# A mixed attention and feed-forward kernel on one core: half of the feed-forward weight loads move to GpSimd's queue

## The chip, the core and the metric

The kernel runs on one core of a Trainium2 chip. Its engines are TensorE (PE, with weight loads shown apart as PEld), VectorE (DVE), ScalarE (ACT), GpSimd (POOL) and SyncE (SP). SP, ACT and POOL can each issue DMAs; all DMAs run on the core's 16 DMA engines. The metric is the device time of one execution in microseconds (us). Times in the profile are counted from the start of the profiled span.

## What is computed

One input x of 2048 rows by 640 columns (bf16) goes through two branches, which a gate mixes per row.

```python
g = _sigmoid((x * gate_w).sum(-1, keepdims=True))
a = _A_ref(x, A_wqkv, A_w_phi, A_wo)      # linear attention, 32 heads of 20
b = (_gelu(x @ w_gate) * (x @ w_up)) @ w_down      # 640 -> 1728 -> 640
return g * a + (1 - g) * b
```

In the attention branch q, k and v come from `x @ wqkv`. q and k go through a 20 by 20 matrix per head (`w_phi`) and then through two softmaxes, of the result and of its negative, so that each head has 40 features. The sums over the rows of features times v, and of the features alone, give numerator and denominator of each row's output, which `wo` maps back to 640 columns.

## The kernel before

**Tiling.** Rows are taken in 16 tiles of 128 and in 4 blocks of 512. The 1728 columns of the feed-forward branch are 13 chunks of 128 and a tail of 64, whose gate and up halves share one tile `wt`. `chunk(b, c)` makes five matmuls of 512 columns with `wg` and five with `wu` (L647), applies GELU on ScalarE (L661) and multiplies on VectorE (L663) into `hT`. `down_tile` (L935, L944) adds the products with `w_down` and those of the attention with `wo` for one tile of rows.

**Startup.** `startup` (L446) loads everything. The first 512 rows of x come as rows (`xtok`) and are transposed on TensorE (`tile`, L559) and copied out by ACT or DVE (L593, L595); the other three blocks of x (`x_t`), and the columns of wqkv that belong to k and q (`w_t`, giving `WkT` and `WT`, six transposes each), come through DMA transposes on SP (L454). `spin` (L550) issues products of zeros on TensorE whose result nobody reads: 18 before the first x tile, five before the first weights. Chunks 0 and 1 of block 0 are made in two halves of 256 rows, because x arrives in parts; chunks 2 to 4 follow with 512 columns.

**The fold.** `w_phi` is folded into the weights of k and q. `masks` (L606) builds, on GpSimd, the block-diagonal matrices `BD` of six groups of six heads from `w6` (the loaded `w_phi`) and the mask `BM`. `fold_m` (L621) multiplies `WkT` (or `WT`) by `BD`: a first half needs groups 0 to 2, a second groups 3 to 5. The results go to `wK` (`wQ`), and `half` (L687) then makes k, v and q of one tile of rows in two halves of 320 columns. `wV` is loaded as it is, with the gate vector as a 641st column; `grow` is the gate vector as five rows, transposed at L573.

**Order.** The kernel does not stand in the order in which it is written. Each step is recorded by `_Prog.op` with an engine, an estimated duration, a priority and what it reads and writes; `schedule` then lays out a queue for each engine from these estimates, and `emit` writes the instructions with semaphore waits. Reads and writes in SBUF are compared in cells of 32 bytes (`CELL`). `TIMES` holds the priorities of the later stages (written as due times), `HOLD` how long a switch of ScalarE's function table is put off. On each engine the instructions run in the order so found, and a waiting instruction holds all that is queued behind it on that engine.

**DMA queues.** Before the change every load is issued by SP, but for the gate row (ACT) and `w_down` and `wo`, which GpSimd issues once the last transpose of `WT` has landed (`after=(tr,)`). In the wait lists a DMA's semaphore belongs to a lane of its queue; SP has 24 lanes, GpSimd 8.

**SP's order before:** two tiles of x, gate and up columns 0 to 256, two tiles of x, gate and up columns 256 to 640, the larger piece of w_phi, six WkT transposes, the smaller piece of w_phi, wV, gate and up columns 640 to 1152, and then transposes of x, between which the remaining gate, up and tail columns stand.

Of the kernel before, what the change touches and what calls it, by code (L numbers as in the profile page):

```python
# [7 lines left out]
P = 128  # L8
# [24 lines left out]
class _Prog:  # L33
# [70 lines left out]
        return o  # L104


    HOLD = 3.9

    def schedule(self):
        ops = self.ops  # L110
# [160 lines left out]
class _Kernel:  # L271
    S, D, H, F = 2048, 640, 32, 1728
    DH, KD, NT, NB, TB, BT = 20, 5, 16, 4, 4, 512
    NG, HPG = 6, 6
# [14 lines left out]
    def alloc(self):  # L289
        nc = self.nc  # L290
        T = nc.alloc_sbuf_tensor
        D, S, KD = self.D, self.S, self.KD
        self.ident = T("ident", [P, P], BF)
        self.KVM = T("KVM", [P, 6, 21], BF)
        self.KV = T("KV", [P, self.NCH, 63], BF)
        self.gcol = T("gcol", [P, self.NT], F32)
        self.Gr = T("Gr", [P, self.NT], F32)
        self.Gm = T("Gm", [P, self.NT], F32)
        self.xT = T("xT", [P, KD, S], BF)
        self.wo = T("wo", [P, KD, D], BF)  # L300
        self.wg = T("wg", [P, KD, self.FM], BF)
        self.wu = T("wu", [P, KD, self.FM], BF)
        self.wt = T("wt", [P, KD, P], BF)
        self.wd = T("wd", [P, self.NC, D], BF)
        self.hT = T("hT", [P, 2, self.NC, self.BT], BF)
        SW = self.HP * self.DH
        self.Sq = T("Sq", [P, self.NT, SW], BF)
        self.NSK = 4
        self.Sk = T("Sk", [P, self.NSK, SW], BF)
        self.NVA = 6  # L310
        self.vaug = T("vaug", [P, self.NVA, self.HP, self.DH + 1], BF)
        self.NGL = 4
        self.gel = T("gel", [P, self.NGL, self.BT], BF)
        self.NOS = 2
        self.osb = T("osb", [P, self.NOS, D], BF)
        self.NSM = 2
        HB = 2 * self.HP
        self.t1 = T("t1", [P, 2, HB, 10], BF)
        self.t2 = T("t2", [P, 2, HB, 4], BF)
        self.t3 = T("t3", [P, 2, HB, 2], BF)  # L320
        self.m2 = T("m2", [P, self.NSM, 2, HB, 2], BF)
        self.rr = T("rr", [P, self.NSM, 2 * HB], F32)
        self.r2 = T("r2", [P, self.NSM, 2 * HB, 2], BF)
        self.zt = T("zt", [P, 4, 18], F32)
        self.zr = T("zr", [P, 4, 18], F32)

        self.NE = 5
        self.dn = T("dn", [P, self.NE, 2 * self.NCH, 6], F32)
        self.E = T("E", [P, self.NE, 2 * self.NCH, P], BF)
        self.e_slot = {}  # L330
        self.e_of = [None] * self.NE
        self.e_left = {}
        self.e_ring = 0
        self.dn_left = [0] * self.NE

        b0 = nc.lookup_mloc(self.hT).addr + self.NC * self.BT * 2
        W = self.HPG * self.DH
        for name, shape in (("BD", [P, self.NG, W]), ("BM", [P, W]),
                            ("w6", [W, self.NG, self.DH]),
                            ("grow", [KD, P])):  # L340
            setattr(self, name, nc.alloc_sbuf_tensor_at(name, shape, BF, offset=b0))
            b0 += -(-int(np.prod(shape[1:])) * 2 // 64) * 64
        b1 = nc.lookup_mloc(self.Sq).addr
        self.xtok = nc.alloc_sbuf_tensor_at("xtok", [P, self.TB, D], BF, offset=b1)
        self.WkT = nc.alloc_sbuf_tensor_at("WkT", [P, self.NG, D], BF, offset=b1 + self.TB * D * 2)
        self.WT = nc.alloc_sbuf_tensor_at("WT", [P, self.NG, D], BF, offset=b1 + (self.TB + self.NG) * D * 2)
        assert self.TB + 2 * self.NG <= self.NT


        wk = T("wK", [P, KD, D], BF)  # L350
        wv = T("wV", [P, KD, D + 16], BF)
        wq = T("wQ", [P, KD, D], BF)
        self.wP = (wk, wq, wv)
        b2 = nc.lookup_mloc(wk).addr
        kv, end = KD * (2 * D + 16) * 2, KD * (3 * D + 16) * 2

        def inside(name, shape, n, at):
            size = int(np.prod(shape[1:])) * 2
            return [nc.alloc_sbuf_tensor_at(f"{name}{i}", shape, BF, offset=b2 + at + i * size) for i in range(n)]
        pt = self.NCH * P * 2  # L360
        self.phiT = inside("phiT", [P, self.NCH, P], 2, 0)
        self.OT = inside("OT", [P, KD, P], 4, 2 * pt)
        assert 2 * pt + 4 * 1280 <= kv
        self.OT += inside("OTq", [P, KD, P], 2, kv)
        self.phiT += inside("phiTq", [P, self.NCH, P], 1, kv + 2560)
        assert kv + 2560 + pt <= end
        self.O = [T(f"O{i}", [P, D], BF) for i in range(2)]
        self.NO, self.NOT = 2, 6
        self.ps = nc.alloc_psum_tensor("ps", [P, 8 * BANK], F32)
# [24 lines left out]
    def at(self, T, fn, *args):  # L394
# [1 line left out]
        self.todo.append((T, len(self.todo), fn, args))  # L396


    TIMES = dict(wkp=-4.57, dfk=0.51, dfq=0.95, mask=-16.43, fold_k=12.18, t0=33.24, per=21.78, pair=3.13,
                 exp=3.84, ff=14.55, dff=2.71, fold_q=39.04, rest=-4.17, drest=-3.34, q=-38.61, dq=2.39,  # L400
                 qlate=13.99, q0pre=-21.12, q0exp=-8.41, q0post=1.5, at0=31.81, d0=53.28, q1pre=-18.21,
                 q1exp=2.34, q1post=25.29, f2=28.62, df=1.8, at1=10.48, d1=41.89, q2pre=4.15, q2exp=7.74,
                 q2post=13.74, f3=67.06, at2=21.14, d2=90.12, q3pre=-29.71, q3exp=6.32, q3post=17.94, at3=41.36,
                 d3=45.04)

    def plan(self):
        q = self.TIMES
# [38 lines left out]
    def startup(self):  # L446
# [4 lines left out]
        def dma(q, dst, src, prio, nbytes, after=(), transpose=False, dur=0.45):  # L451
            def emit(e):
                if transpose:
                    return e.dma_start_transpose(dst, src)  # L454
                return e.dma_start(dst, src)  # L455
            return pr.op(q, emit, writes=[dst], dur=dur, prio=prio, dma=True, nbytes=nbytes, after=after)
# [19 lines left out]
        pool(lambda e: e.affine_select(bmv, bmv, pattern=[[DH, HPG], [0, DH]], compare_op=ALU.is_ge, fill=0.0,  # L476
                                       base=DH - 1, channel_multiplier=-1), [bm], [bm], 120)

        dma("act", self.grow[:, :], self.gw_d.rearrange("(kt p) -> kt p", p=P), -30.0, 2000)
        for t in range(self.TB):  # L480
            dma("sp", self.xtok[:, t, :], self.x2[t * P:(t + 1) * P, :], -9.0 + t, 163840)
        wg_r = self.wg_d.rearrange("(kt p) n -> p kt n", p=P)
# [1 line left out]
        D2 = 2 * D  # L484
        wr = self.wqkv.rearrange("(kt p) n -> p kt n", p=P)

        def ffn_w(i, a, b):
            n = (b - a) * (1420 if b - a < 512 else 1070)
            dma("sp", self.wg[:, :, a:b], wg_r[:, :, a:b], i, n)
            dma("sp", self.wu[:, :, a:b], wu_r[:, :, a:b], i + 0.01, n)  # L490

        ffn_w(-7.5, 0, 256)
        ffn_w(-4.8, 256, 640)

        wphi = self.wphi.rearrange("h d f -> (h d) f")
        W = HPG * DH
        r = self.rows_g[-1]
        dma("sp", self.w6[:, 0:NG - 1, :], wphi[0:W * (NG - 1), :].rearrange("(g p) f -> p g f", p=W), -4.75, 240000)
        dma("sp", self.w6[0:r, NG - 1, :], wphi[W * (NG - 1):, :], -4.74, 20000)
        wkp = self.TIMES["wkp"]  # L500

        def w_t(dst, col, i):
            for g in range(NG):
                c0 = col + g * HPG * DH
                o = dma("sp", dst[:, g, :], self.wqkv[:, c0:c0 + P], i + 0.001 * g, 400000, transpose=True, dur=1.3)
            return o
        w_t(self.WkT, D, wkp)
        dma("sp", self.wP[2][:, :, 0:D], wr[:, :, D2:3 * D], wkp + 0.009, 657000)
        ffn_w(-4.4, 640, 1152)

        def x_t(b):
            for kt in range(KD):
                dma("sp", self.xT[:, kt, b * 512:(b + 1) * 512], self.x2[b * 512:(b + 1) * 512, kt * P:(kt + 1) * P],
                    -4.3 + 0.1 * b + 0.01 * kt, 380000, transpose=True, dur=1.6)
        x_t(1)
        ffn_w(-4.19, 1152, self.FM)
        dma("sp", self.wt[:, :, 0:64], wg_r[:, :, self.FM:self.F], -4.18, 81920)
        dma("sp", self.wt[:, :, 64:128], wu_r[:, :, self.FM:self.F], -4.17, 81920)
        x_t(2)
        tr = w_t(self.WT, 0, -4.05)  # L520
        x_t(3)
# [32 lines left out]
        def tile(t, prio):  # L554
            bk = self.next_a()

            def tr(e):
# [13 lines left out]
        col = self.wP[2][:, :, D:D + 1].rearrange("p k o -> p (k o)")  # L571
        bg = self.next_a()
        pr.op("pe", lambda e: e.transpose(self.bankb(bg, 8)[:, 0:KD], gr, idk), reads=[gr, idk], writes=[bg], dur=0.1,  # L573
              prio=1.4)
        pr.op("dve", lambda e: e.tensor_copy(col, self.bankb(bg, 8)[:, 0:KD]), reads=[bg], writes=[col], dur=0.1, prio=3.5)
        spin(5, 1.5, (tile(1, 1.0),))
        banks = [(_Bank(True), _Bank(True)) for _ in range(2)]
        for h in range(2):
            if h:
# [18 lines left out]
    def masks(self, p0):  # L598

        W = self.HPG * self.DH  # L600
        bm = self.BM[0:W, :].rearrange("p (j f) -> p j f", f=self.DH)
        for g in range(self.NG):
            dst = self.BD[0:W, g, :].rearrange("p (j f) -> p j f", f=self.DH)
            src = self.w6[:, g, :]
            sb = src.unsqueeze(1).to_broadcast([W, self.HPG, self.DH])
            self.pr.op("pool", lambda e, dst=dst, sb=sb: e.tensor_tensor(dst, sb, bm, ALU.mult),  # L606
                       reads=[src, self.BM[0:W, :]], writes=[dst], dur=0.35, prio=p0)
# [393 lines left out]
```

## Time and profile before

| | |
|---|---|
| median of 3 runs | 293.33 us (291.94 to 294.5) |
| the profiled execution | 294.05 us, of which 291.5 us are the profiled span |
| TensorE busy | 285.8 us, 98% of the span |
| VectorE / ScalarE / GpSimd busy | 210.7 / 160.8 / 11.6 us |
| granted TensorE clock | 1.00 throughout |
| DMA | 24.24 MB in 61739 packets, 52803 of them under 512 bytes |

A page's groups are named by line, engine, operation and tiles; "ps<-xT,wg" is a product of xT and wg written to the accumulator ps. Matmuls are pipelined, so the busy time of a group is not the sum of single durations, and the chain (the work that ended last, followed back) gives the better spacing. For a DMA two things are shown: when it is issued, and how long it takes from the issue until its data has landed. The queue q1 in the DMA table is SP's, q0 (software_dynamic) GpSimd's, q10 ACT's. "share of 16 engines" is the time that the packets of a queue took, over that of 16 DMA engines in the window.

### The profile page before, as it was taken

Reading aid. Unit: us, or ns where it says so; the run is one execution under the profiler, and the core shown is the slowest. Engines: PE = TensorE matmul, PEld = TensorE weight load, DVE = VectorE, ACT = ScalarE, POOL = GpSimd, SP = SyncE. Lnnn points to the kernel's source line nnn. Section 1 sums busy time; section 2 is a strip of 40 time slices with the busy share of each in tenths; the row PEclk is TensorE's granted clock in tenths of the full one; section 3 lists DMA queues with packets and bytes.
Section 4 is the critical chain, followed back from the end, with each engine's and each line's share of the span. In section 5 each row is a group of like instructions: output and inputs, shape, how many; then the busy total and the mean of one; then the engine's idle time right before and its main releaser. Section 6 shows DMA issues by size and latency. Waiting matters only on the chain.

```text
span 291.5 us, 5260 instructions
## 1 busy us (share of the span) xinstructions
PE 285.8 (98%) x2123; PEld 180.8 (62%) x2123; DVE 210.7 (72%) x422; ACT 160.8 (55%) x274; POOL 11.6 (4%) x42
## 2 busy tenths in 40 slices
PE   7999999999999999999999999999999999999996
PEld 6747556567766566456577755655665444777775
DVE  1251799999959999999999999999895332623420
ACT  4318597998686599349917725952861223121121
POOL 8210002100000000000000000000000000000000
PEclk9999999999999999999999999999999999999999
DMA  7969956970000000000455364061313000782421
GB/s 207 199 173 329 176 116 115 297 168 0 2 0 2 0 0 3 0 3 7 92 74 117 93 147 66 9 144 47 72 45 74 0 0 2 135 130 74 92 67 45
DMA packets 61739, 24.24 MB, mean 83 GB/s; under 512 B 52803, under 2 KB 61123, under 8 KB 61715
## 3 DMA queue, kind: packets, MB, share of 16 engines
q1 hardware_dynamic: 60921, 20.83, 33.5%
q0 software_dynamic: 640, 3.03, 3.7%
q8 instruction: 16, 0.26, 0.4%
q14 instruction: 8, 0.07, 0.1%
q10 hardware_dynamic: 154, 0.04, 0.1%
HBM read 8.96 MB, written 2.62 MB: 40 GB/s over the span
## 4 chain that ended last, share of the span: by engine, by line
PE 94%; ACT 2%; DMA 1%; DVE 1%; issue 1%; SPq 0%
PE ps L647 39%; PE ps L687 21%; PE ps L935 21%; PE ps L944 7%; PE ps L756 2%; PE ps L892 2%; DMA wg<-in_B_w_gate_dram 1%; ACT E L803 1%; DVE wK L595 1%; PE ps L621 1%; ACT L803 0%; PE ps L559 0%; SPq L455 0%; ACT Sq L593 0%; ACT gel L661 0%
## 5 line engine op out<-in xcount | busy, mean ns | idle before, releaser
L935 PE MATMUL ps<-wd,hT 128*128 128x320 bf16 (+1 forms) x462 | 65.7, 295 | 0.0
L647 PE MATMUL ps<-xT,wg 128*128 128x512 bf16 (+1 forms) x270 | 63.1, 376 | 0.9 <-DMA wg<-in_B_w_gate_dram 0.8
L647 PE MATMUL ps<-xT,wu 128*128 128x512 bf16 (+1 forms) x270 | 62.7, 374 | 0.0
L661 ACT ACTIVATE gel<-ps 128x512 bf16<-128x512 f32 (+1 forms) x56 | 32.6, 597 | 54.0 <-PE ps L647 53.8
L663 DVE TENSOR_TENSOR hT<-ps,gel 128x512 bf16<-128x512 f32 (+1 forms) x56 | 38.5, 688 | 24.1 <-PE ps L647 23.1
L935 PEld LDWEIGHTS ps<-wd,hT 128*128 128x128 bf16 x462 | 43.5, 98 | 16.2
L821 DVE TENSOR_REDUCE dn<-E 128x132 f32<-128x2640 bf16 x16 | 46.3, 2898 | 4.8 <-ACT E L803 4.7
L950 ACT ACTIVATE osb<-ps,Gm 128x320 bf16<-128x320 f32 (+1 forms) x33 | 16.7, 516 | 52.3 <-PE ps L944 52.1
L647 PEld LDWEIGHTS ps<-xT,wg 128*128 128x128 bf16 x270 | 26.3, 99 | 27.5 <-DVE xT L595 1.4
L647 PEld LDWEIGHTS ps<-xT,wu 128*128 128x128 bf16 x270 | 26.3, 99 | 25.9
L803 ACT ACTIVATE E<-E 128x1320 bf16<-128x1320 bf16 x32 | 40.9, 1307 | 0.6 <-DVE E L796 0.5
L687 PE MATMUL ps<-wK,xT 128*128 128x320 bf16 x160 | 25.7, 299 | 0.7 <-DVE wK L595 0.7
L782 DVE TENSOR_TENSOR t<-t 128x132 bf16<-128x132 bf16 (+1 forms) x96 | 25.2, 262 | 1.0
L687 PE MATMUL ps<-wV,xT 128*128 128x321 bf16 (+1 forms) x160 | 25.7, 300 | 0.0
L687 PE MATMUL ps<-wQ,xT 128*128 128x320 bf16 x160 | 24.4, 299 | 0.2 <-ACT Sq L593 0.2
L687 PEld LDWEIGHTS ps<-wK,xT 128*128 128x128 bf16 x160 | 15.5, 98 | 8.1 <-DVE wK L595 0.8
L900 DVE SCALAR_TENSOR_TENSOR zt<-dn,ps 128x18 f32<-128x18 f32 (+1 forms) x32 | 5.4, 167 | 20.8 <-PE ps L892 20.8
L687 PEld LDWEIGHTS ps<-wQ,xT 128*128 128x128 bf16 x160 | 15.4, 98 | 7.2 <-ACT Sq L593 0.6
L687 PEld LDWEIGHTS ps<-wV,xT 128*128 128x128 bf16 x160 | 15.4, 98 | 7.1
L944 PE MATMUL ps<-wo,OT 128*128 128x320 bf16 (+1 forms) x125 | 19.4, 294 | 0.0
L842 DVE TENSOR_TENSOR E<-E,r 128x2640 bf16<-128x2640 bf16 (+1 forms) x16 | 18.8, 1177 | 0.0
L593 ACT ACTIVATE Sk<-ps 128x320 bf16<-128x320 f32 x32 | 13.9, 448 | 7.2 <-PE ps L687 6.9
(80 smaller groups left out, 254.3 us busy)
## 6 DMA issues: line engine op xcount, KB each, us to landing
out_dram<-osb SPq DMA_DIRECT2D x15, 160.0 KB, 1.8
wd<-in_B_w_down_dram POOLq DMA_DIRECT2D x1, 2080.0 KB, 11.8
wg<-in_B_w_gate_dram SPq DMA_DIRECT2D x2, 640.0 KB, 5.9
wu<-in_B_w_up_dram SPq DMA_DIRECT2D x2, 640.0 KB, 6.6
wV<-in_A_wqkv_dram SPq DMA_DIRECT2D x1, 800.0 KB, 4.7
wo<-in_A_wo_dram POOLq DMA_DIRECT2D x1, 800.0 KB, 12.8
xtok<-in_A_x_dram SPq DMA_DIRECT2D x4, 160.0 KB, 3.3
wg<-in_B_w_gate_dram SPq DMA_DIRECT2D x1, 480.0 KB, 5.7
```

The source lines that it names most:

```text
L593: self.pr.op("act", lambda e: e.activation(dst, src(), AF.Copy), reads=[bk], writes=[dst], dur=_act(n), prio=prio)
L647: i = e.matmul(out, w[:, kt, :], x[:, kt, :], start=kt == 0, stop=kt == self.KD - 1)
L661: pr.op("act", lambda e: e.activation(g2, self.bank(pg)[r0, :], AF.Gelu_apprx_tanh), reads=[pg], writes=[gs], dur=_act(512), prio=prio, ta ...
L663: pr.op("dve", lambda e: e.tensor_tensor(h, self.bank(pu)[r1, :], g2, ALU.mult), reads=[gs, pu], writes=[h], dur=_dve(512, 1, True), prio= ...
L687: i = e.matmul(self.bank(bk, n), x[:, kt, :], w[:, kt, :], start=kt == 0, stop=kt == self.KD - 1)
L782: pr.op("dve", lambda e: e.tensor_tensor(o, a, b, op), reads=[a, b], writes=[o], dur=_dve(el, rate), prio=T + q)
L803: self.pr.op("act", lambda e, dj=dj: e.activation(dj, dj, AF.Exp), reads=[dj], writes=[dj], dur=_act(1320), prio=T + 0.01 * j, table="exp")
L821: pr.op("dve", lambda e: e.tensor_reduce(dn, d4, AX.X, ALU.add), reads=[d4], writes=[dn], dur=_dve(20 * H), prio=T)
L842: pr.op("dve", lambda e: e.tensor_tensor(dd, dd, m, ALU.mult), reads=[dd, r2], writes=[dd], dur=_dve(20 * H, 2), prio=T + 0.03)
L935: i = e.matmul(out, self.hT[:, hs, c, j * P:(j + 1) * P], self.wd[:, c, c0:c1], start=c == 0, stop=False)
L944: i = e.matmul(out, ot[:, k, :], self.wo[:, k, c0:c1], start=False, stop=k == self.KD - 1)
L950: pr.op("act", lambda e, dst=dst, bk=bk, n=n, gm=gm: e.activation(dst, self.bank(bk, n), AF.Copy, scale=gm), reads=[bk, gm], writes=[dst], ...
```

## The change

In `startup`:

```diff
-        dma("act", self.grow[:, :], self.gw_d.rearrange("(kt p) -> kt p", p=P), -30.0, 2000)
+        dma("sp", self.grow[:, :], self.gw_d.rearrange("(kt p) -> kt p", p=P), -5.9, 2000)
...
-        def ffn_w(i, a, b):
+        def ffn_w(q, i, a, b, after=()):
             n = (b - a) * (1420 if b - a < 512 else 1070)
-            dma("sp", self.wg[:, :, a:b], wg_r[:, :, a:b], i, n)
-            dma("sp", self.wu[:, :, a:b], wu_r[:, :, a:b], i + 0.01, n)
-
-        ffn_w(-7.5, 0, 256)
-        ffn_w(-4.8, 256, 640)
+            dur = 1.0 if q == "pool" else 0.45
+            return dma(q, self.wg[:, :, a:b], wg_r[:, :, a:b], i, n, after, dur=dur), dma(q, self.wu[:, :, a:b], wu_r[:, :, a:b], i + 0.01, n, after, dur=dur)
+
+        ffn_w("sp", -7.5, 0, 256)
+        p1 = ffn_w("sp", -4.8, 256, 640)
...
-        ffn_w(-4.4, 640, 1152)
+        p2 = ffn_w("pool", -4.4, 640, 1152, p1[:1])
...
-        ffn_w(-4.19, 1152, self.FM)
-        dma("sp", self.wt[:, :, 0:64], wg_r[:, :, self.FM:self.F], -4.18, 81920)
-        dma("sp", self.wt[:, :, 64:128], wu_r[:, :, self.FM:self.F], -4.17, 81920)
+        ffn_w("pool", -4.19, 1152, self.FM, p2[:1])
+        dma("pool", self.wt[:, :, 0:64], wg_r[:, :, self.FM:self.F], -4.18, 81920, p2[1:], dur=1.0)
+        dma("pool", self.wt[:, :, 64:128], wu_r[:, :, self.FM:self.F], -4.17, 81920, p2[1:], dur=1.0)
...
-              prio=1.4)
+              prio=1.8)
...
-        spin(5, 1.5, (tile(1, 1.0),))
+        spin(12, 1.5, (tile(1, 1.0),))
```

Gate and up columns from 640 on (chunk 5 and later) go to GpSimd's queue. The first pair (640 to 1152) is issued after the gate columns 256 to 640 have landed, the second pair (1152 to 1664) after the first pair's gate half, the tail after its up half. The gate row is loaded by SP, behind the four tiles of x, and its transpose moves behind the tiles 2 and 3. Twelve instead of five products of zeros stand before the first weights.

`w6` gets rows of 32 columns of which 20 are used, so that a row fills 64 bytes; the loads and `masks` take the 20 columns:

```diff
-                            ("w6", [W, self.NG, self.DH]),
+                            ("w6", [W, self.NG, 32]),
...
-        dma("sp", self.w6[:, 0:NG - 1, :], wphi[0:W * (NG - 1), :].rearrange("(g p) f -> p g f", p=W), -4.75, 240000)
-        dma("sp", self.w6[0:r, NG - 1, :], wphi[W * (NG - 1):, :], -4.74, 20000)
+        dma("sp", self.w6[:, 0:NG - 1, 0:DH], wphi[0:W * (NG - 1), :].rearrange("(g p) f -> p g f", p=W), -4.75, 240000)
+        dma("sp", self.w6[0:r, NG - 1, 0:DH], wphi[W * (NG - 1):, :], -4.74, 20000)
```

The scheduler's estimates change: a DMA transpose of `w_t` counts as 220000 bytes and 1.31 us instead of 400000 and 1.3, one of `x_t` as 180000 bytes and 1.31 us instead of 380000 and 1.6. `HOLD` goes from 3.9 to 3.6, and the 40 values of `TIMES` are replaced by another set. With these the order on all engines differs. In the built program SP's new order is: two tiles of x, gate and up columns 0 to 256, two tiles of x, the gate row, gate and up columns 256 to 640, both pieces of w_phi, six WkT transposes, wV, ten transposes of x, six WT transposes, five transposes of x. GpSimd issues the first pair behind its memsets, then the six `masks` products, then the second pair, the tail, `w_down` and `wo`. On TensorE the order after the first two chunks is:

```
wg chunk 2, wg chunk 3, wu chunk 2
fold of k x9 (WkT 0 to 2), wu chunk 3, fold x3, wg chunk 4, fold x3
wg chunk 5 (first pair of GpSimd's queue), wu chunk 4, wK x5
fold of k x15 (WkT 3 to 5), wK x10, wV x5
```

Before it was: wg of chunks 2 and 3, wu of both, wg of chunk 4, fold x12, wu of chunk 4, fold x3, wK x15, fold x15, wV x15; chunk 5's gate products stood behind several more products with wK and wV.

## The prediction

> **What bounds the kernel now.** I read the page's busy table first, then the waits of TensorE, then the chain in order of time over the first 26 us, then the DMA queues in windows.
>
> ```profile
> PE 285.8 (98%) x2123; PEld 180.8 (62%) x2123; DVE 210.7 (72%) x422; ACT 160.8 (55%) x274; POOL 11.6 (4%) x42
> ```
>
> TensorE is the bound, so a gain can only be work taken off it, work run at a faster rate, or idle time. The waits (who waited for whom, us, times) show how little idle time there is:
>
> ```profile
> PE ps L550 <- DVE gel L464: 1.1, 1, 1.1
> PE ps L647 <- DMA wg<-in_B_w_gate_dram: 0.8, 1, 0.8
> PE ps L687 <- DVE wK L595: 0.7, 1, 0.7
> PE ps L687 <- ACT Sq L593: 0.2, 1, 0.2
> PE ps L647 <- ACT wQ L593: 0.2, 1, 0.2
> ```
>
> After the first weights only 1.1 us of waits are left, nearly all before 21.1 us. The chain in order of time (start, length, what) shows a second loss:
>
> ```profile
> 5.80 2.29 PE ps L647 x10
> 8.09 0.53 PE ps L559 x5
> 8.62 1.07 PE ps L647 x5
> 9.69 0.48 PE ps L559 x5
> 10.17 0.55 PE ps L647 x5
> ...
> 18.71 2.30 DVE wK L595 x5
> ```
>
> The same five 256-column products take 1.07 us at 8.62 and 0.55 us at 10.17: TensorE runs at half rate until about 10 us. Were the 15 products and 10 transposes of 5.8 to 10 us at full rate they would be shorter by 15 x 0.105 + 10 x 0.05 = 2.1 us. So the most that this change can win is near 2.1 + 1.1 us plus some 0.2 us for which the second half's first product waits on L595 at 10.7: 3.4 us, 1.2% of the span. A loss has no such limit, and it is decided in the DMA queues. Three windows, 34 to 37, 52 to 55 and 57 to 62 us (packets, MB, share of 16 engines):
>
> ```profile
> q1 hardware_dynamic: 1639, 0.39, 60.2%
> ```
> ```profile
> q0 software_dynamic: 206, 1.05, 98.8%
> q1 hardware_dynamic: 21, 0.00, 0.4%
> ...
> xT<-in_A_x_dram SPq DMA_TRANSPOSE x2, 12.7
> ```
> ```profile
> q0 software_dynamic: 261, 1.17, 95.7%
> q1 hardware_dynamic: 261, 0.07, 6.5%
> ```
>
> q1 is SP's queue, q0 GpSimd's. Alone, SP's transposes move 1639 packets in 3 us, 546 a us. While GpSimd's load of w_down and wo runs (issued at 49.03), they move 7 a us, and later 52 a us, one for each packet of q0; but a packet of q0 carries 4.5 KB or more and one of a transpose some 250 bytes. Those transposes landed after 12.7 us, against 2.7 us in 34 to 37. This is the row that decides the case.
>
> **The change part by part.**
>
> *Useless products, 5 to 12.* They begin at 4.24 us; at 117 ns each (L550: 18 in 2.10 us) twelve end near 5.64, just before the weights land at 5.71. They cost nothing while that wait lasts 1.4 us, and without it up to 0.8 us more than the five. What they may win is an earlier full rate: between 0 and 2.1 us (above); I take 0 for the sum, as 18 products from 1.06 us and five at 4.24 did not bring it before 10 us.
>
> [...]
>
> *Gate row on SP behind x.* Its transpose (0.1 us) leaves the front and stands behind the tiles 2 and 3. Its issue, about 0.5 us (w_phi's small piece took 0.51), delays what SP issues behind it: gate/up columns 256 to 640, w_phi, WkT. The data of the former wait in a full queue anyway (5 to 9 us runs at over 300 GB/s), so their landing (issued 3.80, 5.7 us to land, 9.5) moves little, 0 to 0.5 us.
>
> *w_phi rows padded to 64 bytes.* The 20-column rows shared 32-byte cells, so the second piece stood behind the first: issued at 17.08, after six WkT transposes. Now both go out together and SP reaches the WkT transposes 0.5 us later; with the gate row about 1.0 us in all. GpSimd's last two masks (19.03, 0.88 us) come forward to about 13.5; nobody waited for them.
>
> *Gate/up of chunks 5 and on to GpSimd.* SP loses six issues (0.52 + 0.53 + 0.58 + 0.58 + 0.52 + 0.58 = 3.3 us) from between its transposes of x. GpSimd gains them: 0.91 us each by its wo row. The first waits for gate columns 256 to 640 (9.5 to 10.0), so the pair is issued by 11.4 to 11.9, and only then come the six masks (w_phi landed at 11.3; six by 0.37 us: done near 14). The second pair waits for the first's gate half. In between stands TensorE's new order: chunks 2 and 3 gate, chunk 2 up, then nine fold products that need WkT 0 to 2, later six (and nine) that need WkT 3 to 5, then wV. It also runs chunk 5's gate before the keys.
>
> When TensorE arrives without any stall: before, fold at 18.35, second fold 22.97, wV 23.80. The new order has 1.4 us less work ahead of the fold (three 512-column groups instead of five and the fold's place: 13.0 against 14.4 us by row means, of which 0.75 are the new useless products in an idle stretch), 0.5 us more ahead of the second, 1.8 more ahead of wV. Taking off the 0.2 us at 10.7 and the 0.7 us wait for wK: arrivals at about 16.0, 21.8 and 24.0 us, and an end 0.9 us earlier than before.
>
> When the data land: before, WkT 2 is issued at 10.75 and lands 4.7 us later, 15.4; WkT 5 at 18.8; wV (17.63 + 4.7) at 22.3. Now add GpSimd's transfers. w_down's first packets came 2 us after its issue, so the first pair moves from about 11.8. A pair is 1.3 MB; at 52 to 69 packets a us and 4.5 KB a packet 3.8 to 5 us, so to about 16; the second follows after a gap of 0 to 1 us and ends near 20.5 to 21.5, with the tail weights. In such a stretch a WkT transpose (640 rows of 256 bytes, so 640 packets) gets 7 to 60 a us instead of 546. At 11.8 us WkT 1 lacks some 350 packets and WkT 2 all 640. Four us of the first pair give at most 240, a gap of 1 us some 550, the rest comes at 60 a us: WkT 2 lands between 17 (gap of 1 us) and 22 us (no gap and 7 a us), and I take 19.3, nearest the one-for-one row. WkT 3 to 5 follow at 546 a us from 21: 24; wV (800 KB) 2.5 us behind, 26.5.
>
> The sum: 19.3 - 16.0 = 3.3 us of stall at the fold; the second fold then is reached at 25.1 and wV at 27.3, behind their data, so nothing is added. Less the 0.9 us: +2.4 us. All behind it is bound by TensorE and moves with it. The span becomes 291.5 + 2.4 = 293.9; the profiled execution took 294.05, 2.55 outside the span, so 296.45; the median of the runs lies 0.7 below it: 293.33 + 2.4 = **295.7 us**. Bounds of the landing, 17 to 22 us: +0.1 to +5.1.
>
> [...]
>
> *HOLD and TIMES.* These reorder everything behind 25 us. The counts of products and table loads stay (22 loads in each). Attention's first product stands at 141.5 us of TensorE's summed work, before at 140.2; the last tiles' within 1 us of before. Later waits were 0.4 us; the new ones may be 0 to 2 us, and I take 0.4, unchanged.
>
> **The rivals.**
> - *The transposes come through* (faster). WkT 2 lands by 16.0 us: it did at 15.4, so the margin is 0.6 us and is eaten by SP's 1.0 us later start unless GpSimd's packets come later than 13 us. Then the end is 0.9 us earlier, and an earlier full rate adds at most some 0.6, because WkT 2 and wV then end the waits: 292.4, or 291.8. For it: q1's transposes already in the rings at 11.8 us. Against it: the two windows above. Chance 0.24.
> - *Full starvation*. WkT 2, issued about 11.3, needs 12.7 us like the transposes of x: 24.0. The stall is 8.0 us, +7.1: 300.4, and a TensorE idle for so long may fall back to half rate. It decides if GpSimd's two pairs leave no gap. Against it: the second pair has to wait for the first's landing. Chance 0.17.
> - *The new order stalls later*: VectorE, busy 97.3 of 100 us in 100 to 200, becomes late for attention. 1 to 4 us, 294 to 297. Against it: the places of the summed work above. Chance 0.07.
>
> **How the numbers follow.** My forecast has the remaining 0.52. A change of about 1% (2.9 us) is what a measurement of this kernel can tell from none; its three runs differ by 2.6 us. Of the forecast's band (+0.1 to +5.1) a little under half, 0.25, lies above +2.9; with 0.17 and 0.04 of the third rival slower is 0.46. The first rival could pass -2.9 only with the full 2.1 us and no DMA wait: 0.08 faster. Same is the rest, 0.46. The range takes in the first rival down to 291.0 and the second's lower half up to 299.0.
>
> **What would show it.** In the new profile: a wait of TensorE at L620 for DMA WkT of 2 to 5 us between 15 and 21 us; WkT landings over 6 us; q1 at one packet for each of q0 between 12 and 20. The first rival shows itself by no such wait and a fold near 16. If 256-column products run at 0.11 us each before 8 us, the useless products did turn the clock. I am wrong if q0's packets turn out small, or if SP's transposes land in 3 to 5 us beside them.

## The result and the profile after

| | before | after |
|---|---|---|
| median of the runs taken together | 293.6 us (4 runs, 291.94 to 294.5) | 298.03 us (4 runs, 295.79 to 303.74) |
| ratio, 95% interval | | 1.0151 [1.0105, 1.0197] |
| profiled execution, its span | 294.05, 291.5 us | 297.25, 295.1 us |
| TensorE busy | 285.8 us | 287.2 us |

The changed kernel is slower by 1.5%. All ratios here leave out runs that lie more than 1.5% above the fastest of their kernel, so they understate the changed kernel's spread.

The waits of TensorE in the profile after (who waited for whom, us in total, times, longest):

```profile
PE ps L686 <- DMA wV<-in_A_wqkv_dram: 2.1, 1, 2.1
PE ps L620 <- DMA WkT<-in_A_wqkv_dram: 1.9, 1, 1.9
PE ps L549 <- DVE gel L463: 1.1, 1, 1.1
```

The list has no others. The wait for the first weights (0.8 before) and those for wK, Sq and wQ (1.1 together) are gone; two waits for data of SP's queue stand in their place. TensorE's timeline (start, length, what, in brackets the idle time before it):

```profile
8.25 1.27 PE L646 MATMUL ps<-xT,wu 128*128 128x256 bf16 x10
...
16.81 0.65 PE L620 MATMUL ps<-BD,WkT 120*128 120x120 bf16 x9 [1.87 <-DMA WkT<-in_A_wqkv_dram]
...
26.92 0.96 PE L686 MATMUL ps<-wV,xT 128*128 128x320 bf16 x4 [2.08 <-DMA wV<-in_A_wqkv_dram]
```

The first line answers to the 1.07 us that five such products took before: now ten take 1.27, so the clock is full by then. The trace's clock record has its first entry, full clock, at 6.77 us here and at 9.98 before, 3.2 us apart. (Ahead of that entry the views print 1.00 all the same, so the "1.00 throughout" of the kernel before does not hold for its first 10 us, in which the products ran at half rate.) The chain of waits after, and then the piece of the chain before that is the same work:

```profile
17.46 9.41 DMA wV<-in_A_wqkv_dram
26.87 0.05 issue
26.92 8.65 PE ps L686 x50
...
36.65 2.04 PE ps L686 x15
```
```profile
23.91 6.86 PE ps L687 x50
```

wV took 4.7 us from issue to landing before and 9.4 now. The 50 products behind it take 8.65 us in place of 6.86, though the 15 further on run at the old pace (0.136 us each, so 50 would be 6.8). Windows of TensorE (window, us, busy us, products, granted clock, DMA share, GB/s) show why:

```profile
13.60:17.01 3.41, 1.54 (x11) 1.00 1.09 341
23.84:27.25 3.41, 1.33 (x11) 1.00 1.11 281
27.25:30.66 3.41, 3.41 (x15) 0.50 0.64 140
30.66:34.07 3.41, 3.41 (x27) 1.00 0.58 116
```

For 3.41 us behind the wait for wV the clock is at half.

**Where the 3.6 us of span come from.** The first product with wV stands at 26.92 us; before it stood at 23.80. It now has chunk 5's gate products (1.08 us) ahead of it, so 3.12 - 1.08 = 2.04 us are lost up to there: two waits of 3.95 us, less some 1.9 us that TensorE had gained (the earlier clock, the 0.7 us for wK). The half clock costs 8.65 - 6.8 = 1.85 us. Together 3.9; what follows gives 0.3 back.

The DMA table in two windows of the profile after, 17 to 19 us and 19 to 21 us (packets, MB, share of 16 engines), where q0 is GpSimd's queue:

```profile
q1 hardware_dynamic: 1927, 0.48, 107.1%
q0 software_dynamic: 36, 0.08, 11.9%
```
```profile
q0 software_dynamic: 200, 0.75, 107.1%
q1 hardware_dynamic: 10, 0.00, 0.5%
```

In the gap of 1.8 us between GpSimd's two pairs SP's transposes move 964 packets a us. Behind 19 us SP's queue moves 5 a us, but these are not transposes held up: the trace's packet records have 640 packets of 256 bytes for each WkT transpose, and all 3840 had moved by 19.0 us. What then waits is the completion of WkT 5, which landed only at 22.3 (before, the landing came 0.5 us behind its last packet), and wV, whose first packet moved 4.4 us after its issue (21.82 against 17.46; before 1.1 us, 18.69 against 17.63). Transposes are held up earlier, by the first pair: WkT 2's packets took from 12.44 to 15.39 us, 2.95 us in place of 1.16 (12.11 to 13.27 before). From 13 to 14 us the table has one row:

```profile
q0 software_dynamic: 64, 0.26, 89.6%
```

WkT 3 and 4 (landed at 18.4 and 19.0) slipped through the gap; WkT 5's landing (22.3) and wV (26.9) fell under the second pair.

### The profile page after: what moved, and what is told of

It reads as the page before. It is cut to its first block, busy times and chain, and to the rows that moved or that the text cites. A ratio compares the mean times of both kernels' runs of the same rounds, so it can differ in the third digit from the quotient of the medians.

```text
span 295.1 us, 5273 instructions
## 1 busy us (share of the span) xinstructions
PE 287.2 (97%) x2130; PEld 181.1 (61%) x2130; DVE 211.2 (72%) x422; ACT 161.4 (55%) x274; POOL 16.8 (6%) x48
## 3 DMA queue, kind: packets, MB, share of 16 engines
HBM read 8.96 MB, written 2.62 MB: 39 GB/s over the span
## 4 chain that ended last, share of the span: by engine, by line
PE 89%; SPq 4%; DMA 3%; POOL 2%; ACT 1%; issue 0%; POOLq 0%
PE ps L646 35%; PE ps L686 22%; PE ps L934 21%; PE ps L943 7%; SPq L453 3%; DMA wV<-in_A_wqkv_dram 3%; PE ps L755 2%; PE ps L891 2%; SPq L454 1%; ACT L660 0%; PE ps L620 0%; ACT wQ L592 0%; POOL E L530 0%; ACT gel L660 0%; POOL wd L534 0%
## 5 line engine op out<-in xcount | busy, mean ns | idle before, releaser
L646 PE MATMUL ps<-xT,wu 128*128 128x512 bf16 (+1 forms) x270 | 62.0, 371 | 0.0
L662 DVE TENSOR_TENSOR hT<-ps,gel 128x512 bf16<-128x512 f32 (+1 forms) x56 | 37.9, 683 | 27.9 <-PE ps L646 24.4
L686 PE MATMUL ps<-wV,xT 128*128 128x321 bf16 (+1 forms) x160 | 26.3, 303 | 2.1 <-DMA wV<-in_A_wqkv_dram 2.1
L686 PE MATMUL ps<-wK,xT 128*128 128x320 bf16 x160 | 27.0, 310 | 0.1
L686 PE MATMUL ps<-wQ,xT 128*128 128x320 bf16 x160 | 25.2, 299 | 0.0
L686 PEld LDWEIGHTS ps<-wV,xT 128*128 128x128 bf16 x160 | 15.3, 99 | 8.9 <-DMA wV<-in_A_wqkv_dram 2.4
L592 ACT ACTIVATE Sq<-ps 128x320 bf16<-128x320 f32 x32 | 14.0, 449 | 10.8 <-PE ps L686 10.7
L686 PEld LDWEIGHTS ps<-wQ,xT 128*128 128x128 bf16 x160 | 15.4, 98 | 6.8
L592 ACT ACTIVATE vaug<-ps 128x320 bf16<-128x320 f32 x32 | 14.1, 452 | 8.8 <-PE ps L686 8.6
```

What stands on the lines that cost most here:

```text
L592: self.pr.op("act", lambda e: e.activation(dst, src(), AF.Copy), reads=[bk], writes=[dst], dur=_act(n), prio=prio)
L646: i = e.matmul(out, w[:, kt, :], x[:, kt, :], start=kt == 0, stop=kt == self.KD - 1)
L662: pr.op("dve", lambda e: e.tensor_tensor(h, self.bank(pu)[r1, :], g2, ALU.mult), reads=[gs, pu], writes=[h], dur=_dve(512, 1, True), prio= ...
L686: i = e.matmul(self.bank(bk, n), x[:, kt, :], w[:, kt, :], start=kt == 0, stop=kt == self.KD - 1)
```

## The experiments

The theory after this profile: GpSimd's packets hold up SP's transposes and wV, the waits for them cost about 2 us net, and idle time inside a wait turns the clock down for another 1.8. The main rival: the new order of the work (HOLD, TIMES) costs the time, and the queue little. A landing is always the time at which a transfer's completion was signalled.

**Loads of columns 640 and on back on SP, in the changed kernel**

```diff
-        p2 = ffn_w("pool", -4.4, 640, 1152, p1[:1])
+        p2 = ffn_w("sp", -4.4, 640, 1152)
```

(the second pair and the tail likewise)

> The changed kernel with the gate and up loads of chunks 5 and on back on SP's queue, without their waits; the 12 useless products, the gate row, the padded w_phi rows, HOLD, TIMES and the new estimates stay. (The scheduler then puts chunk 5's gate products behind the keys again.) Theory (GpSimd's packets starve SP's transposes): the wait for WkT at the fold is gone or under 0.5 us, WkT 2 lands near 15.5, wV near 22 to 23 us, no wait for wV over 0.5 us, the clock stays full from about 7 us; span 289.5 to 291, so 291 to 293 us, as fast as before or up to 0.8% faster. Rival A (SP's later start of the WkT transposes, by gate row and w_phi, is what costs): WkT 2 still lands after 16.5 us, span about 294. Rival B (the new TIMES order stalls by itself): waits of 2 us or more remain elsewhere, span 294 or more.

Measured 298.97 us, ratio 1.0211 [1.0145, 1.0278], span 297.3. Its waits of TensorE:

```profile
PE ps L686 <- DMA wV<-in_A_wqkv_dram: 1.9, 1, 1.9
PE ps L646 <- ACT gel L660: 1.9, 1, 1.9
...
PE ps L646 <- ACT Sq L592: 1.0, 1, 1.0
```

WkT 2 landed at 14.5 and wV at 22.5, early as expected; the total was missed. The order is laid out from estimates, so an edit to a load moves work on every engine, and the priorities were not made for that: TensorE came to wV at 20.6, before its data, and the waits for ScalarE are new. Of the 257 us behind 40 us TensorE was idle for 6.4. By its span the run looks like rival B, but its order is not that of the changed kernel: it shows what the queue does to the landings and settles nothing of the total. It also shows that a wait for wV of 1.9 us can come from the order, with no load of GpSimd's in flight.

**GpSimd's first pair only when wV has landed**

```diff
-        dma("sp", self.wP[2][:, :, 0:D], wr[:, :, D2:3 * D], wkp + 0.009, 657000)
-        p2 = ffn_w("pool", -4.4, 640, 1152, p1[:1])
+        wvl = dma("sp", self.wP[2][:, :, 0:D], wr[:, :, D2:3 * D], wkp + 0.009, 657000)
+        p2 = ffn_w("pool", -4.4, 640, 1152, (wvl,))
```

> The changed kernel with the loads still on GpSimd's queue, but the first pair is issued only after wV has landed. Its order on TensorE up to 40 us is that of e1. Theory (it is the time at which GpSimd's packets run, beside the WkT transposes and wV, and not the queue): fold and wV as in e1, span 289.5 to 291.5; the transposes of x behind wV are starved in its place (5 to 10 us to land), which is hidden, as x's second block is needed at about 39 us. Rival (GpSimd's queue is slow in itself, whatever runs beside it): chunk 5's gate products wait for the first pair, 1 us or more, and the span is 293 or more.

Measured 301.57 us, ratio 1.0257 [1.0195, 1.0319], span 299.9. The order changed here too (up to 40 us it is that of the run above), with the same new waits for ScalarE. Landings again early: WkT 2 at 14.6, wV at 23.0. TensorE waited 2.4 us for wV, and the clock was at half from 23.7 to 27.2; in the run above 1.9 us at the same place did not turn it down (that run has no clock record; its ten products behind the wait took 1.54 us, the full rate). The rival's span came out, but not its sign: TensorE's waits have none for the weights of GpSimd's queue.

**The kernel before with twelve useless products**

```diff
-        spin(5, 1.5, (tile(1, 1.0),))
+        spin(12, 1.5, (tile(1, 1.0),))
```

> The kernel before with 12 useless products in place of 5, nothing else. Theory (the longer run of products turns the clock up earlier): full clock near 6.8 us in place of 10.0, TensorE reaches the fold about 1.1 to 1.5 us earlier, no later wait for WkT (15.4), and the wait for wV (22.3) stays under 0.7 us: span 290 to 290.8, 0.2 to 0.5% faster. Rival (the window of the clock runs freely and the place of its edge is chance): full clock between 6.5 and 10 us, the span within 0.2% of before.

Measured 291.97 us (10 runs, 291.38 to 292.33), ratio 0.9965 [0.994, 0.999], span 290.1. Its timeline:

```profile
5.98 1.65 PE L647 MATMUL ps<-xT,wg 128*128 128x256 bf16 x10 [0.25 <-issue]
...
8.18 1.25 PE L647 MATMUL ps<-xT,wu 128*128 128x256 bf16 x10
```

Full clock from 6.8 us in place of 10.0. This edit alone wins 1.2 us, and of all kernels run, this is the fastest. One profile cannot refute the rival, that the place of the edge is chance; the first profile of the changed kernel, with twelve products too, has the edge at 6.77 us, that of the kernel before, with five, at 9.98.

**The kernel before with GpSimd's loads** (the six loads of the diff, with the change's waits)

> The kernel before with the loads of chunks 5 and on on GpSimd's queue, with the waits that the change gives them; 5 useless products, gate row on ACT, unpadded w_phi, old TIMES. Theory: a wait for WkT at the fold of 0.5 to 2 us, wV landing near 26 to 28 us and a wait for it of 1 to 3 us, span 293.5 to 296, as slow as the changed kernel (0.7 to 1.5% over before). Rival (other parts of the change cost the time): span 291 to 292.5.

Measured 309.39 us, ratio 1.0518 [1.0435, 1.0602], span 305.7. WkT 2 landed at 16.8, WkT 5 at 25.2, wV at 30.1 (10.7 us from its issue), with a wait of 2.1 us and half clock behind it. But here too the order was laid anew, and 6.7 us of waits of TensorE for ScalarE are its own:

```profile
PE ps L687 <- DMA wV<-in_A_wqkv_dram: 2.1, 1, 2.1
PE ps L687 <- ACT Sk L593: 1.8, 1, 1.8
PE ps L647 <- ACT Sk L593: 1.7, 2, 1.1
PE ps L647 <- ACT Sq L593: 1.6, 1, 1.6
PE ps L621 <- ACT gcol L593: 1.6, 1, 1.6
```

In the kernels that follow, the edit leaves the order that `schedule` found for TensorE, VectorE and ScalarE as it is.

**Second pair held until wV has landed, order kept**

```diff
         order = self.schedule()
+        for o in self.pair2:
+            o.preds.add(self.wv)
```

> The changed kernel with every engine's order of work as it is; only GpSimd's second pair of loads (columns 1152 and on) additionally waits until wV has landed, and what GpSimd issues behind it comes that much later. Theory (the packets of GpSimd's loads hold up SP's; the second pair costs WkT 3 to 5 and wV, the first pair costs WkT 1 and 2): WkT 2 lands at about 16.8 us as before and TensorE still waits about 1.9 us for it at L620; WkT 5 and wV land some 3 us earlier, wV by 24, so the wait of 2.1 us at L686 goes to under 0.5 us, and with it the stretch of half clock behind 27 us. Together about 3.5 us: span 291 to 292. Rival (the half clock comes from the summed idleness, the wait at L620 with it, and not from the wait for wV): the half clock stays, somewhere in 17 to 31 us, and the span is 293 to 294. Rival (SP's transposes are slow by their later start alone): wV still lands after 26 us and the span stays near 295.

Measured 296.18 us, ratio 1.0109 [1.0072, 1.0146], span 293.9. WkT 5 landed at 20.1 and wV at 23.6, and the wait for wV is gone, as expected. That wait proves little, because TensorE, late from the fold, came to wV only at 27.4, by when it had landed in both profiles of the unaltered kernel too (26.9 and 27.3). The fold, with which the edit has nothing to do, waited longer than in the first profile:

```profile
17.97 1.08 PE L622 MATMUL ps<-BD,WkT 120*128 120x120 bf16 x9 [2.97 <-DMA WkT<-in_A_wqkv_dram]
```

WkT 2 landed at 17.9 where the changed kernel's first profile has 16.8, from the same transfers. And the clock fell behind this wait (half from 17.8 to 21.2). The span and the half clock of the first rival came out, for another reason than the rival's: one wait of 3.0 us, not the sum of two.

**GpSimd's gate and up loads cut to 32 columns of each piece, order kept**

```diff
+                if cut:
+                    return e.dma_start(dst[:, :, 0:cut], src[:, :, 0:cut])
```

(the kernel leaves out the other 15/16 of these weights, and its products of chunks 5 and on use those of chunks 0 to 4)

> The changed kernel with every engine's order of work as it is; GpSimd's loads of gate and up columns 640 and on are issued where they were, with 32 columns of each piece only, so that nearly none of their bytes move; the products of chunks 5 and on use the weights of chunks 0 to 4 in their place. Theory (bytes on GpSimd's queue cost the time, not its issues, nor the new order of the work): WkT 2 lands at 14.5 to 15.5 us, wV at about 22.5, TensorE waits under 0.5 us for either, its clock stays full from 6.8 us, and the span is 290 to 291, below the kernel before. Rival (the new order of the work, HOLD and TIMES, costs the time later on): no wait at L620 or L686 either, but the span is 293 or more. Rival (the later start of SP's transposes): WkT 2 still lands after 16 us.

Measured 292.44 us, ratio 0.9997 [0.998, 1.0014], span 290.8. From its page, its waits and its DMA issues:

```profile
PEclk9999999999999999999999999999999999999999
```
```profile
PE ps L623 <- DMA WkT<-in_A_wqkv_dram: 0.8, 1, 0.8
```
```profile
wV<-in_A_wqkv_dram SPq DMA_DIRECT2D x1, 800.0 KB, 6.3
```

wV landed at 23.3 and nobody waited for it. With the bytes of one queue gone, 1.5% are gone, the whole of the loss. The rival of the new order falls: it stands in full in this kernel. WkT 2 still landed at 16.3, 0.8 us behind TensorE; the expectation of 14.5 to 15.5 missed that, and the sign of the third rival (a landing after 16) is there, for a wait of 0.8 us and no loss in the total. What the run shows is the cost of these bytes at this time; no run moved them on SP's queue at the same time.

**The kernel before, order kept, its loads of columns 640 and on moved to GpSimd's queue**

```diff
+        order = rest[:at] + list(p2) + rest[at:later] + [*p3, *tail] + rest[later:]
```

(p2, p3: the two pairs; the last two masks come behind p3 and the tail)

> The kernel before with the order of work of TensorE, VectorE and ScalarE as it is; only the six loads of columns 640 and on go from SP's queue to GpSimd's, with the waits and the place that the change gives them (the last two masks behind the second pair). Theory (the queue alone costs the time): WkT 2 lands 1 to 3 us after its 15.4 us of before, but the fold here is reached at 18.35 us, so at most 0.5 us is waited for it; wV lands at 25 to 28 in place of 22.3 and is waited for by 1.5 to 4 us (reached at 23.8), with a stretch of half clock behind it if the wait is near 2 us or more: span 293.5 to 297. Rival (the order around the fold is what costs, not the queue): under 0.5 us of new waits and the span within 0.6 of the kernel before, 291 to 292.

Measured 304.84 us, ratio 1.0428 [1.0389, 1.0467], span 303.2, far above the range expected. Its timeline:

```profile
20.11 0.81 PE L634 MATMUL ps<-BD,WkT 120*128 120x120 bf16 x12 [1.27 <-DMA WkT<-in_A_wqkv_dram]
...
30.06 1.35 PE L634 MATMUL ps<-BD,WkT 120*128 120x120 bf16 x15 [5.03 <-POOL BD L619]
...
33.48 0.96 PE L700 MATMUL ps<-wV,xT 128*128 128x320 bf16 x3 [2.06 <-DMA wV<-in_A_wqkv_dram]
```

WkT 2 landed at 20.1 and wV at 33.3, the latest of all. The 5.0 us for BD have a cause that the change itself avoids: w_phi's smaller piece, unpadded here, was issued behind the transposes at 19.55, and landed behind the second pair's bytes; the last two masks waited for it until 29.1. So the padding of w_phi, priced at nothing, spares the changed kernel this wait. As a price of the queue alone this run is spoiled.

**The changed kernel with 5 useless products, order kept; the changed kernel unaltered; 5 products once more**

```diff
-                for _ in range(n):
+                for _ in range(5 if n == 12 else n):
```

> The changed kernel with every engine's order of work as it is, and 5 useless products in place of 12. Theory (what the twelve win by an earlier full clock is swallowed by the waits for WkT and wV, which end when their bytes land): the clock is full from about 10 us, not 6.8; the fold is reached about 1.2 us later, near 16.1, the wait at L620 is 0.5 to 0.9 us, wV is waited for by 1 to 2 us, and the span is within 0.5 of the changed kernel's, or below it if the shorter wait for wV no longer turns the clock down (293 to 295). Rival (the twelve still win their 1.2 us or more): 1 to 1.5 us above the changed kernel.

Measured 303.09 us, the median of four runs (298.99 to 304.54), for which no ratio is on record; span 300.6. That is 5 us above the first four runs of the changed kernel, outside what either theory gave. WkT 2 landed at 19.2 (fold wait 3.3) and wV at 32.0, 13.5 us from its issue. Here the transposes are held up packet for packet: WkT 5's 640 packets took from about 20.9 to 25.0 us, and the DMA table from 22 to 24 us is

```profile
q0 software_dynamic: 91, 0.34, 85.4%
q1 hardware_dynamic: 86, 0.02, 5.3%
```

As seven products cannot do that to a DMA queue in any way that the trace shows, both kernels were run again side by side.

> The changed kernel unaltered, for more runs of it and a second profile. Its packets up to 14 us are those of the kernels with the second pair late and with 5 products, whose profiles showed WkT 2 at 17.9 and 19.2 us where the first profile of the changed kernel has 16.8. Theory (which packets get through beside GpSimd's is settled anew in each execution, so that landing, waits and half clock vary): WkT 2 lands anywhere in 16.5 to 20 us and wV in 24 to 32; runs spread over 5 us or more, against 2 for the kernel before; the median is 297 to 301. Rival (the changed kernel's landings are fixed, and the kernel with 5 products lands its data late for a reason of its own): WkT 2 within 0.5 of 16.8, wV within 1 of 26.9, runs within 3 us of each other around 297.

> The changed kernel with 5 useless products in place of 12, once more, beside the unaltered one on the same chip. Theory (the twelve are worth little, because waits for DMA end after them in any case): the medians of the two differ by under 1.5 us and their runs overlap. Rival (the twelve win by more than their 1.2 us, because an earlier TensorE also puts ScalarE's and VectorE's work elsewhere beside GpSimd's loads): 3 us or more above the unaltered one, with wV again after 30 us.

The unaltered kernel gave 298.59 us (295.95 to 302.73, 6 runs), ratio 1.0185 [1.0133, 1.0238]; that with 5 products 298.85 (297.38 to 300.29, 6 runs), ratio 1.022 [1.018, 1.0259]. The two are not told apart, and their landings vary from one execution to the next: the unaltered kernel had WkT 2 at 16.8 in its first profile and at 17.6 in this one, that with 5 products at 19.2 and 16.7, wV at 32.0 and 28.7. In the unaltered kernel's two profiles wV came at 26.9 and 27.3. TensorE's windows, first of the unaltered kernel's second profile, then of the first and the second with 5 products:

```profile
14.74:18.15 3.41, 0.79 (x12) 1.00 1.11 282
18.15:21.56 3.41, 3.41 (x13) 0.50 1.13 337
```
```profile
29.86:33.27 3.41, 1.44 (x11) 1.00 0.90 214
33.27:36.68 3.41, 3.41 (x15) 0.50 0.57 110
```
```profile
23.74:27.16 3.42, 2.18 (x25) 1.00 1.06 288
27.16:30.57 3.41, 1.82 (x14) 1.00 1.06 266
30.57:33.98 3.41, 3.41 (x27) 1.00 0.47 94
```

In the first, all 2.6 us of idle time stand at the fold, in one window, and the next runs at half clock; behind it nothing waits, and the span is 293.8. In the last, a wait of 2.8 us for wV is cut in two by the end of a window, and the clock stays full.

**Sixteen useless products ahead of each of the two waits, order kept**

```diff
+                if keep and p.dma:
+                    self.spin(o.banks[0])
```

> The changed kernel with every engine's order of work as it is, and 16 more useless 128-column products (0.9 us at full rate) just ahead of each of the two waits, for WkT 2 at the fold and for wV. The data come when they come; only the idle time in the waits is 0.9 us shorter. Theory (2.1 us of idleness in one 3.4 us stretch of the clock's record is what turned it down, 1.9 us did not): where the waits left are under 1.5 us the clock stays full behind them and the span is 1.5 to 2 us below that of an execution of the changed kernel with the same landings, 293.0 to 293.7 with those of its first profile. Rival (the clock falls on a count of real work, or by chance): half clock all the same, span 295 or more.

Measured 298.0 us, ratio 1.0173 [1.0115, 1.0231]. In the profiled execution WkT 2 landed at 19.1, so that 3.6 us of wait were left at the fold in spite of the products, and the clock fell; span 297.5. At wV the sixteen left 0.7 us, and the clock stayed full there. Two other executions of it show the full clock (0.999 and 1.0 over the span) and spans of 294.2 and 294.3, for which no landings are on record. Whether the products pay is left open.

**First pair cut to 32 columns, second whole, order kept**

> The changed kernel with every engine's order of work as it is; only GpSimd's first pair (columns 640 to 1152) is cut to 32 columns of each piece, the second pair and the tail are whole; the products of chunks 5 to 8 use the weights of chunks 0 to 3 in their place. Theory (each pair delays what SP has in its queue beside it): WkT 2 lands by 16.3 us as with both pairs cut, the wait at L620 is under 1 us; the second pair, 1 us or more earlier, still holds up WkT 5 and wV: wV lands at 25 to 28 and is waited for by 1.5 to 4 us, with a half clock behind 2 us: span 292.5 to 295.5. Rival (the first pair did all the harm, what follows is its echo): wV by 24, under 0.5 us of wait, span near 291.

Measured 297.09 us, ratio 1.0137 [1.0098, 1.0176], span 294.4. Its timeline:

```profile
15.33 0.65 PE L623 MATMUL ps<-BD,WkT 120*128 120x120 bf16 x9 [0.55 <-DMA WkT<-in_A_wqkv_dram]
...
23.96 1.35 PE L623 MATMUL ps<-BD,WkT 120*128 120x120 bf16 x15 [2.67 <-DMA WkT<-in_A_wqkv_dram]
```

WkT 2 landed at 15.3. The second pair, now earlier, caught WkT 5 (23.9; expected was that the wait would fall on wV, at 27.8) and turned the clock down in the same way. The span lies in the range expected. Either pair alone does harm: 1.1% with the first in its place and the second held, 1.4% with the second alone.

**All profiles together.** Times are us; the idle time is that of the TensorE window that ends where the clock fell, or else of the idlest window.

| kernel | WkT 2 issued, landed | wV issued, landed | idle of 3.41 us | clock behind |
|---|---|---|---|---|
| before | 10.75, 15.4 | 17.63, 22.3 | 0.7 | full |
| before, 12 products | 10.57, 14.2 | 17.03, 21.9 | 0.7 | full |
| loads back on SP | 10.93, 14.5 | 16.81, 22.5 | 1.9 at most | full |
| first pair behind wV | 10.98, 14.6 | 16.89, 23.0 | 2.4 | half |
| both pairs cut | 11.03, 16.3 | 16.94, 23.3 | 0.8 | full |
| first pair cut | 10.31, 15.3 | 16.23, 27.8 | 2.5 | half |
| second pair held | 10.51, 17.9 | 18.11, 23.6 | 2.8 | half |
| after, two profiles | 10.34, 16.8; 10.47, 17.6 | 17.46, 26.9; 18.04, 27.3 | 2.08; 2.6 | half |
| after, 5 products, two profiles | 10.57, 19.2; 10.82, 16.7 | 18.49, 32.0; 17.64, 28.7 | 3.0 and 1.97; 1.6 | half, twice; full |
| after, 16 products at the waits | 10.23, 19.1 | 18.77, 30.9 | 3.2 | half |
| before, loads on GpSimd, new order; order kept | 10.73, 16.8; 10.83, 20.1 | 19.41, 30.1; 20.11, 33.3 | 2.15; 2.2 | half |

With the whole first pair on GpSimd's queue WkT 2 took 5.9 to 9.2 us from issue to landing, in eight profiles; with the pair cut 5.0 and 5.3, without it 3.6 to 4.7. wV took 9.2 to 13.5 us with the second pair beside it and 4.7 to 6.3 without, with no overlap between the two groups.

## Why the prediction was right, and where it was off

The forecast was 295.7 us by a stall of TensorE for WkT, caused by GpSimd's packets. That cause is shown: both pairs cut to a sixteenth, with the order of the work as it was, take the whole loss away (0.9997). The measured loss is 1.5% and 1.85% in two measurements, 4.4 to 5.4 us of 293, against +2.4 forecast. Runs of the changed kernel lie between 295.79 and 303.74 us, so the span of one execution says little. The second profile's span, 293.8, is the forecast's 293.9 by luck: its landing came 1.7 us before the forecast's (17.6 against 19.3), and the half clock, which the sum did not have, took up to 1.7 us. In the first profile the landing came 2.5 us before the forecast's, and a second wait (2.1) and the half clock (1.85) added more than that. Step by step:

- **Useless products, taken at 0 in bounds of 0 to 2.1.** Mis-sized. They gave 1.2 us in the kernel before. The reason for the 0 was that 18 and then five products had not brought the full clock before 10 us. The 3.41 us ahead of the clock's step differ in idle time: before, 0.8 us of it stood between the five and the first weights, and the products behind 6.6 us still ran at half rate; with twelve, 0.25 us stood there, and the clock was full from 6.8. In the changed kernel the gain is not measurable (1.0185 and 1.022, overlapping): it ends in waits for DMA.
- **SP reaches the WkT transposes 1.0 us later.** Right for the first, wrong for those that count. WkT 0 is reached 1.5 us later (7.32 against 5.79), but its issue took 1.42 us in place of 3.47, and WkT 2 was issued at 10.34, before at 10.75.
- **WkT 2 at 19.3, bounds 17 to 22.** It landed between 16.7 and 20.1 in the eight profiles, with a mean of 18.0, three of them just below the bound of 17. The mechanism holds; that the landing differs from one execution to the next was not foreseen. The working has two slips: 1.3 MB at 4.5 KB and 52 to 69 packets a us take 4.2 to 5.6 us, not 3.8 to 5, and its own rates with a gap of 1 us give 19.4 or later, not 17. In the first profile the first pair took 5.9 us (11.3 to 17.2) and the gap was 1.8.
- **Packets one for one.** Only partly. In the first profile q0 moved 64 packets from 13 to 14 us and q1 none, from 14 to 16 us 144 and 665, and in the gap between the pairs all went to SP. One for one, 91 and 86, came in the first profile with 5 products (22 to 24 us).
- **3.3 us of stall at the fold.** 1.9 in the first profile, 2.6 in the second, 3.3 and 0.3 with 5 products. TensorE arrived at 14.94, not at 16.0, through the earlier clock.
- **"wV is reached behind its data, so nothing is added."** This step failed. wV was to land at 26.5 and came at 26.9 and 27.3, but TensorE, stalled 1.4 us less at the fold and 1.1 us earlier there, came to it at 24.84: a second wait of 2.1 us. In the second profile the stall at the fold was longer and nothing was waited for at wV, as forecast.
- **No price for the clock behind a wait.** Named under full starvation only, for an 8 us stall. It came with 2.08 us, and costs up to 3.41 / 2 = 1.7 us; in the first profile 1.85 by the 50 products. This is the term that the sum lacked in both profiles of the changed kernel.
- **HOLD and TIMES, later waits unchanged.** Held: no wait of TensorE behind 27 us in the first profile, and with both pairs cut the kernel is at 0.9997, against 0.9965 for the twelve products alone; that leaves 0.9 us for the order, of which 0.8 is the fold's wait.

Of the rivals, "the transposes come through" is refuted by the eight landings at 16.7 and later. Full starvation did not happen to WkT 2, but did to WkT 5 and wV, which took 12.8 and 13.5 us in the first profile with 5 products.

What sets the landings of an execution is open. The profiles with WkT 2 at 19.1 or later are also those with wV at 30.9 or later, so one early slip seems to carry on; that is a pattern in three profiles and no cause.

## What to carry to other kernels

Moving a load to another engine's queue takes its issue off the first engine (six issues, 3.3 us here) and puts its packets beside those of the first queue: before such a move, compare the packet sizes (4096 against 256 bytes here) and ask which small transfer on the path is in flight at that moment. Price an idle stretch of TensorE twice, by its length and by what the clock does in the 3.4 us behind it (2.08 and 1.85 us at wV in the first profile after). And where a scheduler lays out the order, make an experiment behind it, or what is measured is the new order.

## What the runs showed of the hardware

**The clock.** In the first profile after, the record of the granted clock has steps at 6.77, 27.25 and 30.66 us, 20.48 us (6 x 3.413) and 3.413 us apart. In other executions they stand elsewhere: the first at 9.98 us before, one at 18.15 in the second profile after. Measured by windows, stretches of 3.41 us that end with a step or a multiple of 3.413 us from one: behind 2.08 us of idle time (first profile after), 2.62 us (second) and 1.97 us (first with 5 products) the clock was at 0.50 for the next 3.41 us; behind 1.87 us (first profile after, 13.60 to 17.01) and 1.91 us (the kernel with the first pair behind wV, at 136 us) it stayed full. In the second profile with 5 products the wait of 2.8 us lay in two windows with 1.24 and 1.59 us of idle time, and the clock stayed full. At the start, the kernel before ran at half rate behind a window with 0.82 us of idle time (3.15 to 6.57) and at full clock behind the next, which had none; with twelve products it ran at full clock behind a window with 0.25 us (3.41 to 6.82). The idle times are worked out from the records of the products and of the clock. What the clock does between these cases is not shown.

**Two queues.** Beside GpSimd's packets of 4096 bytes the 640 packets of one WkT transpose took 2.95 us (WkT 2, first profile after) and 4.1 us (WkT 5, first profile with 5 products), against 1.16 us alone (WkT 2 before) and 0.96 and 1.03 us with the first pair cut (WkT 2); between GpSimd's two pairs 964 a us moved (17 to 19 us). Landings came later than the data: WkT 5's 3.3 us behind its last packet after (19.0, 22.3), 0.5 before. Six issues (3.3 us before) left SP, and the transfers got in each other's way: from 14 to 16 us of the first profile after, q0 and q1 took 71.3% and 37.2% of the same 16 engines.

**The same program, other landings.** With two queues at work, WkT 2 of one program landed 2.5 us apart in two executions and wV 3.3 us (5 products). In the five profiles with SP's queue alone up to 22 us or with GpSimd's loads cut, of five different kernels, wV landed within 1.4 us (21.9 to 23.3); how far one such kernel's landings spread is not shown.
